# 256 rows of w_out loaded apart, on engines' queues of their own, in a decode step of attention and a gated MLP

## The chip, the cores and the metric

One core of a Trainium2 chip runs the whole kernel. The metric is the time of one execution on the device, in microseconds; the median of three runs is given, and one execution was taken apart by the hardware profiler. All times below are microseconds, from the start of the profiled span, unless ns is written.

## What is computed

One token `x` (576 numbers) is normalised; an attention block and a gated MLP read the same normalised row, and both results are added to `x`. Cut to what matters:

```
xn = layernorm(x)                                # 1 x 576
# A: 32 query heads on 16 key/value heads, the last 4096 of 65536 positions, heads of 128
q = xn @ wq;  p = softmax(q k^T / sqrt(128));  o = p v
a = o @ wo                                       # 4096 -> 576
# B: gated MLP; w_in is 576 x 4608, w_out is 2304 x 576
z = gelu(xn @ w_in);  z1, z2 = halves of z       # 2304 each
g = w_sp * layernorm(z2) + b_sp                  # w_sp and b_sp are single numbers here
b = (z1 * g) @ w_out
out = x + a + b
```

All inputs are bfloat16. Every weight and every cache row is read once: 51 MB for one row of 576 numbers.

## The kernel before

The heads are taken in four groups of four. For each group b, `turn(b)` transposes the keys on VectorE (eight instructions, L214), `scores(b)` multiplies them with the queries, finds the maximum and takes the exponential (L259 to L285), and `weigh(b)` and `heads(b)` sum the values (L293 to L307). The order is written out by hand at the end of the kernel: turn, scores and values of groups 0 to 2 interleaved, then `turn(3)`, `scores(3)`, `z_all`, `weigh(2)`, `gate`, `heads(2)`, then the first output products, `values(3)`, and the rest of the output products.

The big loads are all issued by SyncE (SP), in this order: `wq` in two, `k0`, `k1`, `v0`, `k2`, `v1`, `k3`, `win`, `v2`, `v3`, `wo` in two, `w_out` in four. They go into two pools of two buffers each, so that a load is issued when the tile that held its buffer has been read: `wo` waits for `win` (read by `z_all`), the tile `wout` for `k3` (read by `turn(3)`). An engine's instructions, the loads that it issues included, run in the order written. A load is split over DMA engines; sixteen serve this core.

`w_out` has 2304 rows; row f needs element f of the hidden vector `hv`. The kernel puts 2304 - 128 = 2176 of them on 128 partitions, 17 rows (FR) on each, and SP loads these in four pieces of 8, 6, 2 and 1 rows per partition (L124). The other 128 rows (FE) stand in further columns of the same tile. ScalarE loads them: 96 rows on 12 partitions, eight rows each (L382), and 32 rows on 32 partitions, one each (L383). Those 96 rows are read so that partition 4i + x gets the rows of block i of the x-th quarter.

`z_all` computes `xn @ w_in` as 9 accumulation steps. In each, eight matmuls write four groups of 32 PSUM partitions, two tiles; the elements that belong to the separate rows stand ahead of the first group's. VectorE copies the result to `zs` and transposes blocks of 32x32, so that each element comes to the partition that holds its row of `w_out` (L333 to L338). GpSimd clears the unused part of `zs` and of `zt`. `gate` then makes `hv`.

The output is one row, built in two PSUM tiles by matmuls with a single column as weights: `row_of` adds one column of `hv` (or of the attention's output `o_p`) times the matching 576 numbers, two matmuls of 288 each (L394). It is called for `x`, then for the columns of the separate rows, then, after `values(3)`, for the 32 columns of `wo`, and last for the 17 columns of `w_out`. Then come two copies and two stores of half a row each.

Of the kernel before, what the change touches and what calls it, by code (L numbers as in the profile page):

```python
# [8 lines left out]
FP32 = mybir.dt.float32  # L9
# [5 lines left out]
P = 128  # L15
D = 576
# [5 lines left out]
FH = 2304  # L22
# [6 lines left out]
NR = 9  # L29
EPS = 1e-5  # L30
SCALE = DH ** -0.5
GELU_C = 0.7978845608028654
FE = P
FR = (FH - FE) // P
FX = 8
FB = 12 * FX
FC = FR + FX + 1
FQ = P * FR // 4
FW = FQ // 2
WR = HQ * DH // P  # L40
HW = D // 2
ZPAD = 24
# [6 lines left out]
def kernel(  # L49
# [14 lines left out]
    nc = tc.nc  # L64
    ctx.enter_context(tc.manual_schedule())

    const = ctx.enter_context(tc.tile_pool(name="const", bufs=1))
    work = ctx.enter_context(tc.tile_pool(name="work", bufs=2))
    one = ctx.enter_context(tc.tile_pool(name="one", bufs=1))
# [7 lines left out]
    ps_a = ctx.enter_context(tc.tile_pool(name="ps_a", bufs=2, space=PS))  # L77


    x_row = const.tile([1, D], BF16, name="x_row")  # L80
    nc.scalar.dma_start(x_row[:], A_x.flatten_outer_dims())
    ws2 = const.tile([1, 2], BF16, name="ws2")
    nc.scalar.dma_start(ws2[:, 0:1], B_w_sp.flatten_outer_dims()[0:1, 0:1])
    nc.scalar.dma_start(ws2[:, 1:2], B_b_sp.flatten_outer_dims()[0:1, 0:1])
# [3 lines left out]
    def unit(name, width):  # L88
        pool = small if width == SMALL else large
        return pool.tile([P, width], BF16, name=name, tag="u")  # L90
# [4 lines left out]
    def load(t, view, width, cuts):  # L95
        for a, e in zip(cuts, cuts[1:]):
            nc.sync.dma_start(t[:, (a - cuts[0]) * width:(e - cuts[0]) * width], view[:, a * width:e * width])
# [19 lines left out]
    win_t = unit("win", LARGE)  # L117
# [3 lines left out]
    wo_t = unit("wo", LARGE)  # L121
    load(wo_t, wo_v, D, (0, 20, WR))
    wout_t = unit("wout", SMALL)
    load(wout_t, B_w_out[FE:FH, :].rearrange("(p r) n -> p (r n)", r=FR), D, (0, 8, 14, 16, FR))  # L124


    ident = const.tile([P, P], BF16, name="ident")
# [1 line left out]
    xw = const.tile([P, NR, 32], BF16, name="xw")  # L129
# [91 lines left out]
    for r in range(NR):  # L221
        for g in range(4):
            nc.tensor.matmul(q_ps[32 * g:32 * g + 32, :], lhsT=xw[:, r, :],  # L223
                             rhs=wq_t[:, 2048 * r + 512 * g:2048 * r + 512 * (g + 1)],
                             start=r == 0, stop=r == NR - 1, tile_position=(0, 32 * g))
# [5 lines left out]
    for g in range(4):  # L231
        nc.tensor.matmul(qr[:, :, g, :], lhsT=rep4[:, g, :, :].rearrange("p n q -> p (n q)"),
                         rhs=qT[:, :, 0:2, :].rearrange("p a h e -> p h a e"), start=True, stop=True)
# [17 lines left out]
    def scores(b):  # L251
        sm = one.tile([P, 2, 512], FP32, name=f"sm{b}", tag="sm")
        mx = work.tile([P, 2], FP32, name=f"mx{b}", tag="mx")
        for kk in range(2):
            s_ps = ps_s.tile([P, 512], FP32, name=f"s{b}_{kk}", tag="s")
            for k4 in range(4):
                for ce in range(4):
                    c, e = divmod(ce, 2)
                    nc.tensor.matmul(s_ps[:], lhsT=zq[:, b, ce, ZPAD - 8 * k4:ZPAD - 8 * k4 + P],  # L259
                                     rhs=kt[b, 4 * kk + k4][:, c, :, e],  # L260
                                     start=k4 == 0 and ce == 0, stop=k4 == 3 and ce == 3)
            nc.vector.tensor_tensor_reduce(  # L262
                out=sm[:, kk, :].rearrange("p (n s) -> p n s", s=HB),
                in0=s_ps[:].rearrange("p (n s) -> p n s", s=HB),
                in1=cm[:].unsqueeze(1).to_broadcast([P, P, HB]), scale=SCALE, scalar=-3e38,
                op0=ALU.add, op1=ALU.max, accum_out=mx[:, kk:kk + 1])
        m1 = work.tile([P, 1], FP32, name=f"m1{b}", tag="m1")
        nc.vector.tensor_max(m1[:], mx[:, 0:1], mx[:, 1:2])  # L268
        tr = ps_m.tile([P, P], FP32, name=f"tr{b}", tag="m")
        nc.tensor.matmul(tr[:], lhsT=m1[:].to_broadcast([P, P]), rhs=ident_f[:], start=True, stop=True)  # L270
        m8 = work.tile([P, 8], FP32, name=f"m8{b}", tag="m8")
        nc.vector.tensor_reduce(out=m8[:], in_=tr[:].rearrange("p (a x) -> p x a", x=8), axis=AXX, op=ALU.max)  # L272
        mj = work.tile([P, 8], FP32, name=f"mj{b}", tag="mj")
        nm = work.tile([P, 1], FP32, name=f"nm{b}", tag="nm")
        nc.vector.tensor_tensor_reduce(out=mj[:], in0=m8[:], in1=sel8[:], scale=-1.0, scalar=0.0,  # L275
                                       op0=ALU.mult, op1=ALU.add, accum_out=nm[:])
        p = one.tile([P, 1024], BF16, name=f"p{b}", tag="p")
        l = work.tile([P, 1], FP32, name=f"l{b}", tag="l")
        nc.scalar.activation(p[:], sm[:].rearrange("p k n -> p (k n)"), ACT.Exp, bias=nm[:], accum_out=l[:])  # L279
        p_t[b] = work.tile([P, 2, 16, 32], BF16, name=f"pt{b}", tag="pt")  # L280
        nc.vector.transpose(p_t[b][:].rearrange("p k u m -> p (k u m)"), p[:])  # L281
        su = ps_m.tile([P, 8], FP32, name=f"su{b}", tag="m")
        nc.tensor.matmul(su[:], lhsT=l[:].to_broadcast([P, P]), rhs=sel8[:], start=True, stop=True)  # L283
        rms[b] = work.tile([P, 8], FP32, name=f"rm{b}", tag="rm")
        nc.vector.reciprocal(rms[b][:], su[:])  # L285
# [23 lines left out]
    def values(b):  # L309
        heads(b, weigh(b))  # L310


    hv = const.tile([P, FC], BF16, name="hv")

    zt = const.tile([P, FC, 32], FP32, name="zt")
    nc.gpsimd.memset(zt[:, FR:, :], 0.0)


    def z_all():
        zs = one.tile([P, FQ + 32 * (FX + 1)], FP32, name="zs", tag="sm")  # L320
        nc.gpsimd.memset(zs[0:32, FQ:], 0.0)
        zx = zs[0:32, FQ:].rearrange("p (r i) -> p r i", i=32)
        zp = [ps_a.tile([P, FE + FW], FP32, name=f"z{i}", tag="a") for i in range(2)]
        for r in range(NR):
            for g in range(4):
                for i in range(2):
                    lead = FE if g == 0 and i == 0 else 0
                    a = FE + FQ * g + FW * i - lead
                    nc.tensor.matmul(zp[i][32 * g:32 * g + 32, FE - lead:], lhsT=xw[:, r, :],  # L329
                                     rhs=win_t[:, FH * r + a:FH * r + a + lead + FW],  # L330
                                     start=r == 0, stop=r == NR - 1, tile_position=(0, 32 * g))
        for i in range(2):
            nc.vector.tensor_copy(zs[:, FW * i:FW * (i + 1)], zp[i][:, FE:])  # L333
        nc.vector.tensor_copy(zx[:, 0:FX, 0:12].rearrange("p r (i x) -> p r i x", x=4),
                              zp[0][0:32, 0:FB].rearrange("p (x i r) -> p r i x", x=4, i=3))
        nc.vector.tensor_copy(zx[:, FX, :], zp[0][0:32, FB:FE])
        nc.vector.transpose(zt[:, 0:FR, :], zs[:, 0:FQ].rearrange("p (i r) -> p r i", r=FR))
        nc.vector.transpose(zt[0:32, FR:, :], zx)  # L338
        return zt[:, :, 0:2]

    def gate(z):
        def t3(name):
            return const.tile([P, FC, 2], FP32, name=name)

# [8 lines left out]
        nc.vector.reciprocal(e[:], e[:])  # L353
        G = const.tile([P, 2, FC], FP32, name="G")
        nc.vector.tensor_mul(G[:].rearrange("p h c -> p c h"), e[:], z)
        sz = const.tile([P, 2], FP32, name="sz")
        nc.vector.tensor_reduce(out=sz[:, 0:1], in_=G[:, 1, :], axis=AXX, op=ALU.add)
        jz = const.tile([P, FC], FP32, name="jz")
        nc.vector.tensor_tensor_reduce(out=jz[:], in0=G[:, 1, :], in1=G[:, 1, :], scale=1.0, scalar=0.0,
# [3 lines left out]
        mz = rstd_of(sp[:], FH, "mz")  # L363
        gz = const.tile([P, FC], FP32, name="gz")
        nc.vector.tensor_scalar(out=gz[:], in0=G[:, 1, :], scalar1=mz[:, 0:1], scalar2=mz[:, 3:4],
# [12 lines left out]
    values(1)  # L378
    turn(3)

    e0 = D * (FR + FX)
    nc.scalar.dma_start(wout_t[0:12, D * FR:e0], B_w_out[0:FB, :].rearrange("(x i r) n -> i x (r n)", x=4, i=3))  # L382
    nc.scalar.dma_start(wout_t[0:32, e0:e0 + D], B_w_out[FB:FE, :])  # L383
    scores(3)
    z = z_all()
    pvs2 = weigh(2)
    gate(z)
# [4 lines left out]
    def row_of(col, w, start=False, stop=False):  # L392
        for g in range(2):
            nc.tensor.matmul(fin[g][32 * g:32 * g + 1, :], lhsT=col, rhs=w[:, HW * g:HW * (g + 1)],  # L394
                             start=start, stop=stop, tile_position=(0, 32 * g))

    row_of(one_bf[:, 0:1], x_row, start=True)
    for r, rows in [(FR + j, 12) for j in range(FX)] + [(FR + FX, 32)]:
        row_of(hv[0:rows, r:r + 1], wout_t[0:rows, D * r:D * (r + 1)])
    values(3)  # L400


# [48 lines left out]
```

## Time and profile before

| | us |
|---|---|
| median of 3 runs | 127.54 (127.38 to 127.61) |
| the profiled execution | 127.4 |
| its span, first to last instruction | 125.6 |
| TensorE busy / VectorE busy / ScalarE busy / GpSimd busy | 77.5 / 64.7 / 10.2 / 4.5 |
| bytes moved | 51.03 MB, mean 406 GB/s |
| granted TensorE clock, mean | 0.864 |

The page gives busy time per engine, the DMA queues (q1 is SP's, q10 ScalarE's, q8 and q14 carry instructions), the chain of work that ended last, and groups of like instructions. PE is TensorE, DVE VectorE, ACT ScalarE, POOL GpSimd, SP SyncE. A line of a timeline has the start, the length, the engine, the source line and operation, the tiles (written from read), the shapes, and in brackets the idle time before with what ended it.

### The profile page before, as it was taken

What the parts mean: (1) busy time and instruction counts of PE and PEld (TensorE: products, weight loads), DVE (VectorE), ACT (ScalarE), POOL (GpSimd) and SP (SyncE); (2) the same over time, 40 slices, a digit from 0 to 9 for tenths busy, and PEclk for the clock granted to TensorE, in tenths of its full rate; (3) what the DMA queues carried; (4) which work ended last, traced back from release to release, by engine and by line L of the source; (5) the groups of instructions that cost most, each with busy time, mean ns of one, the idle gap of its engine ahead of it and who ended that gap; (6) DMA issues with size and microseconds to landing.
All of it is one profiled execution on the core that took longest, in us unless ns stands there. A gap on an engine that the chain in (4) does not pass through costs nothing.

```text
span 125.6 us, 1352 instructions
## 1 busy us (share of the span) xinstructions
PE 77.5 (62%) x546; PEld 37.7 (30%) x550; DVE 64.7 (52%) x132; ACT 10.2 (8%) x19; POOL 4.5 (4%) x12
## 2 busy tenths in 40 slices
PE   3230550099922997385799274997397188749661
PEld 3110220033302342225334033342274063235340
DVE  6660032499648998322998445998326840010001
ACT  4010000000021000310000221000300210100001
POOL 8500000000000000000000000000100000000000
PEclk9999999999985599955579999599958975786999
DMA  4999899898998979999898999989898989999960
GB/s 120 506 438 438 365 470 470 365 501 365 470 459 378 485 344 490 407 428 490 355 490 365 508 423 428 423 384 490 358 462 372 487 359 444 448 395 423 396 249 0
DMA packets 2526, 51.03 MB, mean 406 GB/s; under 512 B 298, under 2 KB 461, under 8 KB 717
## 3 DMA queue, kind: packets, MB, share of 16 engines
q1 hardware_dynamic: 2450, 50.81, 94.9%
q10 hardware_dynamic: 71, 0.15, 0.3%
q8 instruction: 4, 0.07, 0.2%
q14 instruction: 1, 0.01, 0.0%
HBM read 50.96 MB, written 0.00 MB: 406 GB/s over the span
## 4 chain that ended last, share of the span: by engine, by line
PE 42%; DMA 37%; DVE 11%; ACT 5%; issue 2%; SPq 1%; ACTq 0%
PE s L259 29%; DMA wout<-in_B_w_out_dram 20%; DMA k<-in_A_k_cache_dram 18%; ACT p L279 4%; PE pv L293 4%; DVE kt L214 4%; PE z L329 4%; PE op L304 2%; DVE sm L262 2%; PE tr L270 2%; PE fin L394 1%; DVE pt L281 1%; DVE m L272 1%; ACT pvs L298 1%; PE su L283 1%
## 5 line engine op out<-in xcount | busy, mean ns | idle before, releaser
L259 PE MATMUL s<-kt,zq 128*128 128x512 bf16 x124 | 36.3, 451 | 11.6 <-DVE kt L214 10.8
L214 DVE STREAM_TRANSPOSE kt<-k 128x1024 f32<-128x1024 f32 x32 | 36.4, 1204 | 3.9 <-DMA k<-in_A_k_cache_dram 3.9
L259 PEld LDWEIGHTS <-zq 128*128 128x128 bf16 x128 | 14.5, 113 | 32.4 <-issue 21.4
L293 PE MATMUL pv<-v,pt 128*32 128x512 bf16 x128 | 10.1, 469 | 1.1 <-DMA v<-in_A_v_cache_dram 1.1
L279 ACT ACTIVATE p<-sm,nm 128x1024 bf16<-128x1024 f32 x4 | 4.6, 1148 | 71.9 <-DVE nm L275 71.9
L223 PE MATMUL q_ps<-wq,xw 128*32 128x512 bf16 x36 | 4.2, 627 | 7.2 <-DMA wq<-in_A_wq_dram 4.9
L307 DVE TENSOR_TENSOR o_t<-op,rm 128x8 bf16<-128x8 f32 x4 | 0.7, 164 | 15.1 <-PE op L304 15.1
L281 DVE STREAM_TRANSPOSE pt<-p 128x1024 bf16<-128x1024 bf16 x4 | 5.0, 1245 | 5.4 <-ACT p L279 5.4
L262 DVE CUSTOM_DVE_ANT_1 sm<-s,cm 128x512 f32<-128x512 f32 x8 | 5.4, 671 | 3.5 <-PE s L259 3.5
L304 PE MATMUL op<-selu,pvs 128*128 128x8 f32 x32 | 5.3, 293 | 2.5 <-ACT pvs L298 2.1
L283 PE MATMUL su<-sel,l 128*128 128x8 f32 x8 | 1.8, 293 | 7.6 <-ACT p L279 7.6
L394 PE MATMUL fin<-wo,o_p 128*1 128x288 bf16 x64 | 5.7, 345 | 1.2 <-DMA wo<-in_A_wo_dram 1.1
L304 PEld LDWEIGHTS op<-selu,pvs 128*128 128x128 f32 x32 | 5.0, 236 | 4.6 <-ACT pvs L298 4.2
L418 DVE CAST res<-fin 1x288 bf16<-1x288 f32 x1 | 0.4, 445 | 11.4 <-PE fin L394 11.4
L394 PE MATMUL fin<-wout,hv 128*1 128x288 bf16 (+2 forms) x52 | 4.8, 336 | 2.3 <-DMA wout<-in_B_w_out_dram 2.2
L293 PEld LDWEIGHTS <-pt 128*32 128x32 bf16 x128 | 3.7, 112 | 5.8 <-issue 3.1
L227 DVE CAST q_sb<-q_ps 128x512 bf16<-128x512 f32 x1 | 0.7, 690 | 8.1 <-PE q_ps L223 8.1
L394 PEld LDWEIGHTS <-o_p 128*1 128x1 bf16 x64 | 3.3, 99 | 4.0 <-issue 1.1
L329 PE MATMUL z<-win,xw 128*32 128x272 bf16 (+1 forms) x72 | 4.4, 396 | 0.0
L270 PE MATMUL tr<-ident_f,m 128*128 128x128 f32 x8 | 2.0, 326 | 3.9 <-DVE m L268 3.9
L223 PEld LDWEIGHTS <-xw 128*32 128x32 bf16 x36 | 1.4, 130 | 9.2 <-issue 9.2
L298 ACT COPY pvs<-pv 128x512 f32<-128x512 f32 x4 | 2.3, 585 | 20.2 <-PE pv L293 20.2
(93 smaller groups left out, 41.8 us busy)
## 6 DMA issues: line engine op xcount, KB each, us to landing
k<-in_A_k_cache_dram SPq DMA_DIRECT2D x4, 4096.0 KB
v<-in_A_v_cache_dram SPq DMA_DIRECT2D x4, 4096.0 KB, 29.2
win<-in_B_w_in_dram SPq DMA_DIRECT2D x1, 5184.0 KB
wq<-in_A_wq_dram SPq DMA_DIRECT2D x1, 3584.0 KB, 12.7
wo<-in_A_wo_dram SPq DMA_DIRECT2D x1, 2880.0 KB
wo<-in_A_wo_dram SPq DMA_DIRECT2D x1, 1728.0 KB, 20.8
wout<-in_B_w_out_dram SPq DMA_DIRECT2D x1, 1152.0 KB
wq<-in_A_wq_dram SPq DMA_DIRECT2D x1, 1024.0 KB, 4.7
```

The lines of the kernel that those rows point to most:

```text
L214: nc.vector.transpose(t[:].rearrange("p c n e -> p (c n e)").bitcast(FP32), kn[b][:, UK * DH * k:UK * DH * (k + 1)].bitcast(FP32).rearrang ...
L223: nc.tensor.matmul(q_ps[32 * g:32 * g + 32, :], lhsT=xw[:, r, :], rhs=wq_t[:, 2048 * r + 512 * g:2048 * r + 512 * (g + 1)], start=r == 0, ...
L259: nc.tensor.matmul(s_ps[:], lhsT=zq[:, b, ce, ZPAD - 8 * k4:ZPAD - 8 * k4 + P], rhs=kt[b, 4 * kk + k4][:, c, :, e], start=k4 == 0 and ce = ...
L262: nc.vector.tensor_tensor_reduce(out=sm[:, kk, :].rearrange("p (n s) -> p n s", s=HB), in0=s_ps[:].rearrange("p (n s) -> p n s", s=HB), in ...
L270: nc.tensor.matmul(tr[:], lhsT=m1[:].to_broadcast([P, P]), rhs=ident_f[:], start=True, stop=True)
L279: nc.scalar.activation(p[:], sm[:].rearrange("p k n -> p (k n)"), ACT.Exp, bias=nm[:], accum_out=l[:])
L281: nc.vector.transpose(p_t[b][:].rearrange("p k u m -> p (k u m)"), p[:])
L293: nc.tensor.matmul(pv[32 * g:32 * g + 32, :].rearrange("p (n d) -> p n d", n=4), lhsT=p_t[b][:, kk, u, :], rhs=v4[:, kk, u, :, :], start=k ...
L298: nc.scalar.copy(pvs[:], pv[:])
L304: nc.tensor.matmul(op[:], lhsT=pvs[:, DH * u:DH * (u + 1)], rhs=selu[:, 8 * u:8 * u + 8], start=u == 0, stop=u == 3)
L329: nc.tensor.matmul(zp[i][32 * g:32 * g + 32, FE - lead:], lhsT=xw[:, r, :], rhs=win_t[:, FH * r + a:FH * r + a + lead + FW], start=r == 0, ...
L394: nc.tensor.matmul(fin[g][32 * g:32 * g + 1, :], lhsT=col, rhs=w[:, HW * g:HW * (g + 1)], start=start, stop=stop, tile_position=(0, 32 * g))
```

## The change

- SP's part of `w_out` shrinks from 17 to 16 rows per partition (pieces of 8, 5, 2 and 1), and 256 rows are loaded apart from it.
- ScalarE still loads 96 rows on partitions 0 to 11, eight rows each, but issues this after the exponential of `scores(3)`. Its 32-row load is gone.
- GpSimd loads 160 rows on partitions 64 to 79, ten rows each. Ahead of it and behind it GpSimd issues a short load (`skip`) of 8 and of 4 neighbouring partitions into columns that nothing reads. Before these it clears the ten columns of the separate rows on all 128 partitions.
- The products of the separate rows use all 128 partitions (ten columns), where they used 12 or 32 (nine columns).
- `z_all` has six matmuls in a step instead of eight: four of 512 columns, one of 96 and one of 160. VectorE's copies and transposes follow the new layout.
- `x_row` is loaded in two halves.

```diff
-FE = P
-FR = (FH - FE) // P
-FX = 8
-FB = 12 * FX
-FC = FR + FX + 1
-FQ = P * FR // 4
-FW = FQ // 2
+FR = 16
+FA, RA = 96, 8
+FB, RB = 160, 10
+FE = FA + FB
+FC = FR + RB
+FQ = 512
...
-    nc.scalar.dma_start(x_row[:], A_x.flatten_outer_dims())
+    for a in range(0, D, D // 2):
+        nc.scalar.dma_start(x_row[:, a:a + D // 2], A_x.flatten_outer_dims()[:, a:a + D // 2])
...
-    load(wout_t, B_w_out[FE:FH, :].rearrange("(p r) n -> p (r n)", r=FR), D, (0, 8, 14, 16, FR))
+    load(wout_t, B_w_out[FE:FH, :].rearrange("(p r) n -> p (r n)", r=FR), D, (0, 8, 13, 15, FR))
...
-    zt = const.tile([P, FC, 32], FP32, name="zt")
-    nc.gpsimd.memset(zt[:, FR:, :], 0.0)
...
-        zs = one.tile([P, FQ + 32 * (FX + 1)], FP32, name="zs", tag="sm")
-        nc.gpsimd.memset(zs[0:32, FQ:], 0.0)
+        zs = one.tile([P, FQ + 32 * RB], FP32, name="zs", tag="sm")
+        nc.gpsimd.memset(zs[:, FQ:], 0.0)
...
+        def product(i, g, r, a, n, to):
+            nc.tensor.matmul(zp[i][32 * g:32 * g + 32, to:to + n], lhsT=xw[:, r, :],
+                             rhs=win_t[:, FH * r + a:FH * r + a + n],
+                             start=r == 0, stop=r == NR - 1, tile_position=(0, 32 * g))
...
+                product(0, g, r, FE + FQ * g, FQ, 0)
+            product(1, 0, r, 0, FA, 0)
+            product(1, 2, r, FA, FB, FA)
+        nc.vector.tensor_copy(zs[:, 0:FQ], zp[0][:])
+        for q, n, a, rows, k in ((0, 12, 0, RA, 3), (64, 16, FA, RB, 4)):
+            nc.vector.tensor_copy(
+                zx[q:q + 32, 0:rows, 0:n].rearrange("p r (i x) -> p r i x", x=4),
+                zp[1][q:q + 32, a:a + n * rows].rearrange("p (x i r) -> p r i x", x=4, i=k))
+        zt = one.tile([P, FC, 32], FP32, name="zt", tag="zt")
         nc.vector.transpose(zt[:, 0:FR, :], zs[:, 0:FQ].rearrange("p (i r) -> p r i", r=FR))
-        nc.vector.transpose(zt[0:32, FR:, :], zx)
+        nc.vector.transpose(zt[:, FR:, :], zx)
...
-    e0 = D * (FR + FX)
-    nc.scalar.dma_start(wout_t[0:12, D * FR:e0], B_w_out[0:FB, :].rearrange("(x i r) n -> i x (r n)", x=4, i=3))
-    nc.scalar.dma_start(wout_t[0:32, e0:e0 + D], B_w_out[FB:FE, :])
+    def blocks(a, e, k):
+        return B_w_out[a:e, :].rearrange("(x i r) n -> i x (r n)", x=4, i=k)
+
+    def skip(k, a):
+        nc.gpsimd.dma_start(wout_t[0:k, a:a + 32].rearrange("i (m c) -> i m c", m=2),
+                            B_w_out[0:2 * k, 0:16].rearrange("(m i) n -> i m n", m=2))
+
+    nc.gpsimd.memset(wout_t[:, D * FR:D * FC], 0.0)
+    skip(8, D * FC)
+    nc.gpsimd.dma_start(wout_t[64:80, D * FR:D * FC], blocks(FA, FE, 4))
+    skip(4, D * FC + 32)
     scores(3)
+    nc.scalar.dma_start(wout_t[0:12, D * FR:D * (FR + RA)], blocks(0, FA, 3))
...
-    for r, rows in [(FR + j, 12) for j in range(FX)] + [(FR + FX, 32)]:
-        row_of(hv[0:rows, r:r + 1], wout_t[0:rows, D * r:D * (r + 1)])
+    for r in range(FR, FC):
+        row_of(hv[:, r:r + 1], wout_t[:, D * r:D * (r + 1)])
```

More of the change, by code (lines that the diff above doesn't have):

```diff
@@ L313 @@
     hv = const.tile([P, FC], BF16, name="hv")
-    zt = const.tile([P, FC, 32], FP32, name="zt")
-    nc.gpsimd.memset(zt[:, FR:, :], 0.0)
     def z_all():
-        zs = one.tile([P, FQ + 32 * (FX + 1)], FP32, name="zs", tag="sm")
-        nc.gpsimd.memset(zs[0:32, FQ:], 0.0)
-        zx = zs[0:32, FQ:].rearrange("p (r i) -> p r i", i=32)
-        zp = [ps_a.tile([P, FE + FW], FP32, name=f"z{i}", tag="a") for i in range(2)]
+        zs = one.tile([P, FQ + 32 * RB], FP32, name="zs", tag="sm")
+        nc.gpsimd.memset(zs[:, FQ:], 0.0)
@@ L324, in z_all @@
+        zx = zs[:, FQ:].rearrange("p (r i) -> p r i", i=32)
+        zp = [ps_a.tile([P, FQ], FP32, name=f"z{i}", tag="a") for i in range(2)]
+        def product(i, g, r, a, n, to):
+            nc.tensor.matmul(zp[i][32 * g:32 * g + 32, to:to + n], lhsT=xw[:, r, :],
+                             rhs=win_t[:, FH * r + a:FH * r + a + n],
+                             start=r == 0, stop=r == NR - 1, tile_position=(0, 32 * g))
         for r in range(NR):
             for g in range(4):
[L326 to L336, printed above, removed]
+                product(0, g, r, FE + FQ * g, FQ, 0)
+            product(1, 0, r, 0, FA, 0)
+            product(1, 2, r, FA, FB, FA)
+        nc.vector.tensor_copy(zs[:, 0:FQ], zp[0][:])
```

## The prediction

> **What bounds the kernel now.** I read the chain that ended last, then the queues, then the DMA share over the last microseconds, then the packets themselves. The end of the chain:
>
> ```profile
> 96.78 24.82 DMA wout<-in_B_w_out_dram
> 121.60 0.04 issue
> 121.64 1.43 PE fin L394 x18
> 123.07 0.43 DVE res L418
> ```
>
> The last loads of `w_out` end it, after them come 18 matmuls, a copy and the store. The queues:
>
> ```profile
> q1 hardware_dynamic: 2450, 50.81, 94.9%
> q10 hardware_dynamic: 71, 0.15, 0.3%
> q8 instruction: 4, 0.07, 0.2%
> q14 instruction: 1, 0.01, 0.0%
> ```
>
> SP's queue fills 95% of sixteen engines; ScalarE's carries 0.15 MB. So the end is set by bytes per engine, and by the fullest engine. The end of the stream, in columns us, busy time by engine, clock, DMA share, GB/s:
>
> ```profile
> 119.00:120.00 1.00, 0.49 (x9) 0.35 (x9) 0.00 (x0) 0.00 (x0) 0.00 (x0) 1.00 0.95 387
> 120.00:120.50 0.50, 0.50 (x12) 0.35 (x7) 0.00 (x0) 0.00 (x0) 0.00 (x0) 1.00 1.04 403
> 120.50:121.00 0.50, 0.16 (x4) 0.00 (x0) 0.00 (x0) 0.00 (x0) 0.00 (x0) 1.00 0.58 224
> 121.00:121.40 0.40, 0.00 (x0) 0.00 (x0) 0.00 (x0) 0.00 (x0) 0.00 (x0) 1.00 0.56 213
> 121.40:121.80 0.40, 0.16 (x4) 0.12 (x5) 0.00 (x0) 0.00 (x0) 0.00 (x0) 1.00 0.41 150
> 121.80:122.20 0.40, 0.40 (x10) 0.30 (x8) 0.00 (x0) 0.00 (x0) 0.00 (x0) 1.00 0.33 115
> ```
>
> From 120.5 the share is about a half: some engines are done while others still carry rows that the end waits for. The trace records the sixteen completions of the very last load (one per engine):
>
> ```
> 120.98 121.13 121.16 121.20 121.26 121.28 121.29 121.30 | 121.87 | 122.34 122.50 122.53 122.58 122.62 122.65 122.69
> ```
>
> Eight are early, one is 0.6 late, seven are 1.1 to 1.4 late. The packet records (start, duration, queue, size) say why, because on an engine one packet starts 3 to 4 ns before the last one ends and can be followed. Three late ones carry the `w_out[0:96]` load of L382: twelve packets of 9216 bytes, in three groups of four, which put their engines 1.42 behind (end of `v3` 105.04 against 103.63). Four others each carried one 16 KB packet of q8 (at 42.4, 77.7, 97.5, 116.4; 1.02 to 1.11 us each) and are 1.4 behind since then. The one at 121.87 carried q14's 8 KB packet at 38.6.
>
> **The change, part by part** (engine time, which is what counts here; 9216 bytes take 0.349, so 26.4 bytes per ns).
> - SP's `w_out` goes from 17 to 16 rows per partition: eight packets per engine shrink by 1152 bytes, 8 x 0.044 = 0.35 less on every engine.
> - The 32-row load of L383 goes. It put two 1152-byte packets on every engine: `v2`'s eight packets took 9.98 on engines with nothing else, `v3`'s, behind them, 9.71. So 0.27 less on each.
> - ScalarE's 96 rows stay four packets of 9216 bytes on three engines: nothing gained, nothing lost there.
> - GpSimd's 160 rows: the source is read as 4 of 4, where the 96 rows are read as 3 of 4 and went to three engines; so I take four engines with four packets of 11,520 bytes. 4 x 0.436 = 1.74 by bytes; 1.42 x 1.25 = 1.78 by the measured delay. The trace has no load issued by GpSimd; below, it costs its engines 0.44 each (spread over sixteen), above, 1.78.
> - The two `skip` loads: 32-byte pieces, two per partition; a 1152-byte packet lasts 0.051, so at most 0.1, on engines that have 0.3 to spare in the sum below.
>
> Sum, if those four engines are among the eight early ones: 121.28 - 0.35 - 0.27 + 1.74 = 122.40. The instruction engines come to 122.69 - 0.62 = 122.07, ScalarE's to 121.9. So the last completion moves from 122.69 to 122.40. Call SP's four loads of `w_out` a (8 rows per partition), b (5 after, 6 before), c (2) and d (1). Behind b come 16 matmuls instead of 18 (0.077 each); b lands 1.09 before d (121.60, 122.69 before), so 16 x 0.077 = 1.23 from 121.35 ends at 122.58, and d's last two at 122.40 + 0.33 = 122.73. Before, both ended at 123.02. The gain is 0.29. The profiled run took 127.4 (span 125.6, 1.8 around it); 127.4 - 0.29 = 127.11. The median is 0.14 above that run, so 127.25.
>
> Edits costed at nothing, with their cover:
> - `x_row` in two loads: one issue more on ACT (0.23 to 0.53). The matmuls of L161 start later than 2.05, but their copy waits for DVE until 4.20, and q_ps then waits 4.9 for `wq`. Without that cover it costs the issue time. The extra load shifts which semaphore each load takes: SP's `v0` now waits for the first half of `x_row` (landed at 2.00, `v0` is issued at 2.97), and d for `v2` (landed by 95.9) instead of ScalarE's load (96.9); all are there before SP comes to them.
> - `z_all`: 54 matmuls instead of 72 with the same 20,736 columns (4.4 before); copies and transposes on DVE 2.8 before, about 2.9 after. It releases `win`, on which SP's next load waits (95.44), and the queue still holds `v3` until 103.5: 8 us of cover. The 36 instructions fewer on PE put the fourth q8 packet about 1.5 later; its engine is still busy then.
> - GpSimd's memset of 128x5760 (L391 after): 128x2432 took 2.12 and 128x288 0.34, so 4.9, from 86.1 (when DVE has read `k3`) to 91.0. Queued behind it on GpSimd: three load issues and the memset of `zs`, for which DVE's copies wait; and ScalarE's load (86.12 before), behind which its next work is at 97.98.
>
> The fin matmuls on the separate rows now wait for GpSimd's load, and PE queues in order behind them:
>
> ```profile
> 102.95 2.31 PE L394 MATMUL fin<-wout,hv 12*1 12x288 bf16 x18
> 105.69 3.34 PE L293 MATMUL pv<-v,pt 128*32 128x512 bf16 x32 [0.42 <-DMA v<-in_A_v_cache_dram]
> 112.54 5.78 PE L394 MATMUL fin<-wo,o_p 128*1 128x288 bf16 x64 [1.09 <-DMA wo<-in_A_wo_dram]
> ```
>
> ScalarE's load before was issued at 86.12, its first packet moved at 91.00, its last ended at 95.2, since packets of q1 and q10 alternate. With an issue at 93 the same lag and four turns of 1.65 give 103 to 104 for GpSimd's. PE can stand more: `o_p` is ready at 111.7, 5.78 and 1.15 (the first 16 of `w_out`) lead to 118.6, and load b comes at 121.3. So 2.6 to spare beside `v3` (105.69), and the separate rows may start as late as 105.9.
>
> **Weighed against the row.** DVE can be held by GpSimd:
>
> ```profile
> 1.33 2.39 DVE L140 CAST ident_f<-ident 128x128 f32<-128x128 bf16 x1 [0.20 <-POOL ident masks.py:199]
> 1.52 2.12 POOL L138 MEMSET zq<- 128x2432 bf16 x1
> 3.96 0.32 DVE L156 COPY twice<-ident 64x128 bf16<-64x128 bf16 x1
> ```
>
> The cast took 2.39 and ended 0.08 after the memset, where a copy of the same width took 0.32. The new memset is twice as long and lies over `scores(3)` on DVE (L262 to L275, 87.2 to 89.2); at worst these wait until 91.0, 3 us, which the spare 2.6 and the wait for `v3` just about take. [...]
>
> **The rivals.**
> 1. *The load meets a loaded engine* (the other side). The trace names no engines. If one of the four is an instruction engine (122.58 to 122.69) it ends at 122.69 - 0.62 + 1.74 = 123.81, so 128.66: 1.1 slower. With the q14 engine, 121.87 - 0.62 + 1.74 = 122.99: 127.84. It decides from an engine that is over 0.3 behind the early ones. For: five of the thirteen engines without ScalarE's rows are loaded, and four taken anywhere miss them with 70/715. Against: the first load starts on eight engines at 1.76 to 1.88 and on the others at 2.06 to 2.47. Followed from there, the q14 engine, the q8 engine of 97.5 and one of ScalarE's three are in the first group, five of six early engines that can be followed are in the second; and ScalarE's first engine, which had just moved `x_row`, may be late for that reason. So the loaded ones look like one half of the engines, and a block that starts after a skip of eight lies in the other.
> 2. *The load is spread over sixteen engines*, and the four engines are not what happens. Then each gets 11,520 bytes, 0.44: 122.69 - 0.62 + 0.44 = 122.51, 127.36. For: the other loads with many partitions use all engines. Against: the 96 rows went to three. [...]
> 3. *The load comes late.* [...] Completion at 108 gives 129.4. For: 2 us of margin over an issue that the trace has never shown. [...]
>
> **How the numbers follow.** Forecast 0.63, rival 1 0.17, rival 2 0.07, rival 3 0.13. The measurement can tell 0.2%, 0.26 us. The forecast's own range is 126.9 (the instruction engines at 122.07 bind, and nothing else: 0.62 less) to 127.55 (1.78, and 0.2 for small packets); its centre is just past 0.2%, so I split it 0.39 faster, 0.22 same, 0.02 slower. Rival 2 is 0.02 and 0.05. Rivals 1 and 3 are slower. Sum: 0.41, 0.27, 0.32. For 8 in 10 the range has to take in rival 1: 126.9 to 128.7; rival 3 stays out.
>
> **What would show it.** Right: four packets of 11,520 bytes on each of four engines, last completions of the last load near 122.4 on these and 122.1 on the instruction engines, DMA share high until about 121.5. Wrong: completions at 123.7 (rival 1), sixteen such packets on sixteen engines (rival 2), or a long wait of PE for `wout` before `values(3)` (rival 3).

## The result, and the profile after

The median went from 127.56 (127.36 to 127.81, 7 runs) to 127.06 us (126.97 to 127.11, 7 runs): ratio 0.9961, 95% interval 0.9949 to 0.9973, a gain of 0.50. The profiled execution took 127.1 with a span of 125.3, so 0.3 less than the one of before. Measured again later, the pair gave 127.21 against 127.62, ratio 0.9966 (0.9954 to 0.9978), a gain of 0.41. The forecast was 127.25 (126.9 to 128.7), a gain of 0.29.

The queues of the changed kernel, with packets, MB and share of sixteen engines:

```profile
q1 hardware_dynamic: 2450, 50.66, 94.7%
q0 software_dynamic: 144, 0.19, 0.4%
q10 hardware_dynamic: 25, 0.11, 0.2%
q8 instruction: 4, 0.07, 0.2%
q14 instruction: 1, 0.01, 0.0%
```

SP's queue gave up 0.15 MB, the new queue q0 is GpSimd's, and the instruction packets of q8 and q14 are still there. The end of the chain:

```profile
98.28 23.00 DMA wout<-in_B_w_out_dram
121.32 1.40 PE fin L406 x16
122.72 0.44 DVE res L430
```

Still the loads of `w_out`, now 0.32 earlier (121.32 against 121.64), and 16 matmuls behind them. The end of the stream by windows, columns as before:

```profile
119.00:120.00 1.00, 1.00 (x20) 0.68 (x16) 0.00 (x0) 0.00 (x0) 0.00 (x0) 1.00 0.99 388
120.00:120.50 0.50, 0.50 (x12) 0.35 (x7) 0.00 (x0) 0.00 (x0) 0.00 (x0) 1.00 0.73 279
120.50:121.00 0.50, 0.19 (x4) 0.00 (x0) 0.00 (x0) 0.00 (x0) 0.00 (x0) 1.00 0.74 286
121.00:121.40 0.40, 0.08 (x2) 0.08 (x3) 0.00 (x0) 0.00 (x0) 0.00 (x0) 1.00 0.69 259
121.40:121.80 0.40, 0.40 (x8) 0.27 (x9) 0.00 (x0) 0.00 (x0) 0.00 (x0) 1.00 0.40 138
121.80:122.20 0.40, 0.40 (x8) 0.17 (x4) 0.00 (x0) 0.00 (x0) 0.00 (x0) 1.00 0.05 14
```

From 120.5 to 121.4 the share is 0.74 and 0.69, where it was 0.58 and 0.56: fewer engines are done early; the last window falls from 0.33 to 0.05. The sixteen completions of the very last load, one per engine:

```
120.48 120.56 120.71 120.72 | 121.31 | 121.70 121.75 121.90 121.98 122.10 122.13 122.14 122.26 122.29 122.30 122.35
```

Eight early engines have become four, and the last is at 122.35 (122.69 before; 122.40 was forecast). The other part of the change, on PE and GpSimd (start, length, work, idle before):

```profile
105.93 2.08 PE L406 MATMUL fin<-wout,hv 128*1 128x288 bf16 x16 [1.68 <-DMA wout<-in_B_w_out_dram]
113.97 5.68 PE L406 MATMUL fin<-wo,o_p 128*1 128x288 bf16 x64 [0.28 <-DVE o_p L420]
119.54 1.15 PE L406 MATMUL fin<-wout,hv 128*1 128x288 bf16 x16
121.32 1.36 PE L406 MATMUL fin<-wout,hv 128*1 128x288 bf16 x16 [0.63 <-DMA wout<-in_B_w_out_dram]
...
87.72 4.90 POOL L391 MEMSET wout<- 128x5760 bf16 x1 [83.19 <-DVE kt L214]
...
87.59 0.65 DVE L262 CUSTOM_DVE_ANT_1 sm<-s,cm 128x512 f32<-128x512 f32 x1
88.81 0.69 DVE L262 CUSTOM_DVE_ANT_1 sm<-s,cm 128x512 f32<-128x512 f32 x1 [0.56 <-PE s L259]
```

PE now waits 1.68 for GpSimd's load and has little to spare later (0.63 in front of load b). DVE's maxima under the memset take 0.65 and 0.69, as they did without it (0.65 and 0.69 in before).

### The profile page after: what moved, and what is told of

Its sections match the earlier page's. It is cut to its first block, busy times and chain, and to the rows that moved or that the text cites. A ratio compares the mean times of both kernels' runs of the same rounds, so it can differ in the third digit from the quotient of the medians.

```text
span 125.3 us, 1324 instructions
## 1 busy us (share of the span) xinstructions
PE 77.9 (62%) x528; PEld 39.3 (31%) x532; DVE 65.0 (52%) x131; ACT 10.2 (8%) x19; POOL 11.0 (9%) x15
## 4 chain that ended last, share of the span: by engine, by line
PE 43%; DMA 36%; DVE 10%; ACT 4%; issue 3%; SPq 1%; ACTq 0%
PE s L259 29%; DMA wout<-in_B_w_out_dram 18%; DMA k<-in_A_k_cache_dram 18%; PE pv L293 4%; DVE kt L214 4%; PE z L323 3%; ACT p L279 3%; PE op L304 2%; DVE sm L262 2%; PE tr L270 2%; PE fin L406 1%; PE su L283 1%; DVE pt L281 1%; DVE m L272 1%; ACT pvs L298 1%
## 5 line engine op out<-in xcount | busy, mean ns | idle before, releaser
L259 PE MATMUL s<-kt,zq 128*128 128x512 bf16 x124 | 36.8, 458 | 11.8 <-DVE kt L214 11.1
L259 PEld LDWEIGHTS <-zq 128*128 128x128 bf16 x128 | 14.5, 113 | 33.0 <-issue 22.4
L391 POOL MEMSET wout<- 128x5760 bf16 x1 | 4.9, 4897 | 83.2 <-DVE kt L214 83.2
L293 PE MATMUL pv<-v,pt 128*32 128x512 bf16 x128 | 11.9, 498 | 0.0
L293 PEld LDWEIGHTS <-pt 128*32 128x32 bf16 x128 | 5.7, 119 | 3.8 <-issue 2.4
L406 PE MATMUL fin<-wout,hv 128*1 128x288 bf16 x52 | 5.1, 344 | 2.3 <-DMA wout<-in_B_w_out_dram 2.3
L161 PE MATMUL x_ps<-one_bf,x_row 1*64 1x1 bf16 x9 | 1.2, 248 | 5.6 <-DMA x_row<-in_A_x_dram 5.6
L323 PE MATMUL z<-win,xw 128*32 128x512 bf16 (+2 forms) x54 | 4.4, 448 | 0.0
L406 PEld LDWEIGHTS <-hv 128*1 128x1 bf16 x52 | 2.6, 95 | 4.5 <-issue 3.0
## 6 DMA issues: line engine op xcount, KB each, us to landing
wo<-in_A_wo_dram SPq DMA_DIRECT2D x1, 1728.0 KB, 19.4
```

What stands on the lines that cost most here:

```text
L293: nc.tensor.matmul(pv[32 * g:32 * g + 32, :].rearrange("p (n d) -> p n d", n=4), lhsT=p_t[b][:, kk, u, :], rhs=v4[:, kk, u, :, :], start=k ...
L323: nc.tensor.matmul(zp[i][32 * g:32 * g + 32, to:to + n], lhsT=xw[:, r, :], rhs=win_t[:, FH * r + a:FH * r + a + n], start=r == 0, stop=r = ...
L391: nc.gpsimd.memset(wout_t[:, D * FR:D * FC], 0.0)
```

## The experiments

Two theories: the end is set by the fullest engine, and GpSimd's four engines are ones that have nothing else (the sum of the prediction); against it, that the four would do as well anywhere, or that something else, not the bytes per engine, carries the gain. Engine numbers are not in the trace: they are counted here from the order of GpSimd's loads, each taken to start on the engine after the last one's. This is the author's assumption, which no trace shows by itself. The packets of the change fit it: eight of 64 bytes (and eight of 8) in the first short load, four groups of the rows, four of 64 bytes (and twelve of 8) in the second. That would make sixteen engines in all, and each execution would start at the same one. An instruction engine is one that carries a 16 KB packet of q8. Each ratio is against the kernel before, measured beside it.

**Which four engines.** First the four after four (e1), then the four after twelve (e2):

```diff
-    skip(8, D * FC)
-    nc.gpsimd.dma_start(wout_t[64:80, D * FR:D * FC], blocks(FA, FE, 4))
     skip(4, D * FC + 32)
+    nc.gpsimd.dma_start(wout_t[64:80, D * FR:D * FC], blocks(FA, FE, 4))
+    skip(8, D * FC)
```

> The changed kernel with its GpSimd loads in another order: the short one of 4, then the 160 rows, then the short one of 8. Same bytes, same partitions, same queues; if the short loads place the long one, its four engines are now the fifth to eighth. Theory (the fullest engine sets the end): the engines with instruction packets get 1.74 more, last completion near 123.8 instead of 122.35, time 128.5 (128.3 to 128.8), four of the sixteen completions near 120.6 become eight. Rival (a third queue helps wherever its load falls): 127.06 as before, the same completions.

Measured: 130.76, ratio 1.0244 (1.0229 to 1.0259). The direction was expected, the size not: 2.3 more than 128.5. All engines ended 2 us later than in the change: fourteen at 122.52 to 124.42, where the change has 120.48 to 122.35, and two, which fit instruction engines, at 125.80 and 125.92. The rows themselves moved slowly: GpSimd's packets of 11,520 bytes took up to 0.64 instead of 0.434, ScalarE's of 9216 up to 0.68 instead of 0.349, and SP's packets ran at 19.4 to 22.4 bytes per ns from 96 to 104, where they ran at 26.9 until then.

```diff
     skip(8, D * FC)
-    nc.gpsimd.dma_start(wout_t[64:80, D * FR:D * FC], blocks(FA, FE, 4))
     skip(4, D * FC + 32)
+    nc.gpsimd.dma_start(wout_t[64:80, D * FR:D * FC], blocks(FA, FE, 4))
```

> The changed kernel with both short loads ahead of the 160 rows, so that its engines are the last four. Theory: these are as empty as the four before them, last completion 122.2 to 122.4, time 127.05 within 0.15. Rival (partitions 64 to 79 have engines of their own, and others write them slower): packets of 11,520 bytes longer than 0.434 and a time over 127.3.

Measured: 130.93, ratio 1.0260 (1.0244 to 1.0275). A miss of 3.9 us, and the rival came: packets of 11,520 bytes took up to 0.79, and all engines ended late (122.62 to 125.03, and two at 126.05 and 126.08). How much of this comes from engines that aren't empty is told apart in e5.

**Without the rows (e3), and with more of them (e4).**

```diff
-    nc.gpsimd.dma_start(wout_t[64:80, D * FR:D * FC], blocks(FA, FE, 4))
```

> The changed kernel without the load of the 160 rows (they count as zero; a short load of 4 takes its place). Theory: eight engines complete near 120.5 to 120.7 and idle, the instruction engines bind at 122.1 to 122.3, time 126.85 to 127.05: the load that it leaves out costs 0.0 to 0.2, though it is 184 KB. Rival (the load or its memset and wait on PE is what sets the new time): 126.5 or less.

Measured: 127.05 (126.87 to 127.2), ratio 0.9953 (0.9938 to 0.9968). Eight engines are early again (120.44 to 120.71) and the last is at 122.44. So the 160 rows cost nothing that can be measured (127.05 without them, 127.06 with them): they lie on engines that would wait anyway.

```diff
-FR = 16
+FR = 15
-FB, RB = 160, 10
+FB, RB = 288, 9
...
-    nc.gpsimd.memset(wout_t[:, D * FR:D * FC], 0.0)
...
-    nc.gpsimd.dma_start(wout_t[64:80, D * FR:D * FC], blocks(FA, FE, 4))
-    skip(4, D * FC + 32)
+    nc.gpsimd.dma_start(wout_t[64:96, D * FR:D * FC], blocks(FA, FE, 8))
+    nc.gpsimd.memset(wout_t[0:64, D * FR:D * FC], 0.0)
```

> 384 rows apart: 96 by ScalarE as in the change, 288 by GpSimd on partitions 64 to 95, nine rows each, read as 8 of 4, so on eight engines with four packets of 10,368 bytes; SP's part is 15 rows per partition. GpSimd's load is issued ahead of the memset, which covers partitions 0 to 63 only, and the products use 96 partitions. Theory: every engine loses another 0.35, the eight early ones get 1.57: last completion 121.8 to 122.0, time 126.6 to 126.75. Rival (PE's chain behind the separate rows is next: it had 0.6 left in the changed kernel): 126.9 or more, with load b of w_out landing before PE comes to it.

Measured: 128.34, ratio 1.0059 (1.0041 to 1.0077): slower, a miss. Here the packets were not stretched (10,368 bytes in 0.39 to 0.40), and fourteen engines ended by 122.24; two ended at 123.27 and 123.55, and two were done at 120.26 and 120.58. That fits two instruction engines among the eight after eight: 122.07 of the prediction, 0.35 less for the 16th row, four packets of 0.393 more make 123.3.

**Engine or partition.** The first two runs changed the engines and left the rows on partitions 64 to 79 (packets of up to 0.64 and 0.79), the fourth used eight engines and partitions 64 to 95 (0.39 to 0.40). The expectations of e5 and e6 take it that each engine has partitions that it writes in the 128-partition loads: 80 to 95 for the four engines after twelve, and so 64 to 79 for the four after eight. The packet records name neither engines nor partitions, so this is an assumption of the author's. Two runs cross engine and partition: e5 is e2 with partitions 80 to 95, e6 is the change with partitions 80 to 95 (the diff of e6; e5 has the same on top of e2).

```diff
-        for q, n, a, rows, k in ((0, 12, 0, RA, 3), (64, 16, FA, RB, 4)):
+        for q, n, a, rows, k, c in ((0, 12, 0, RA, 3, 0), (64, 16, FA, RB, 4, 16)):
...
-                zx[q:q + 32, 0:rows, 0:n].rearrange("p r (i x) -> p r i x", x=4),
+                zx[q:q + 32, 0:rows, c:c + n].rearrange("p r (i x) -> p r i x", x=4),
...
-    nc.gpsimd.dma_start(wout_t[64:80, D * FR:D * FC], blocks(FA, FE, 4))
+    nc.gpsimd.dma_start(wout_t[80:96, D * FR:D * FC], blocks(FA, FE, 4))
```

> GpSimd's loads in the order skip 8, skip 4, load (as in the run in which the load came last), but the 160 rows on partitions 80 to 95 instead of 64 to 79. Theory: a load issued by GpSimd runs at full rate when each engine writes the partitions that it also writes in the 128-partition loads (the four engines after twelve: 80 to 95 on the upper half), and stretches otherwise. Then the 11,520-byte packets are back at 0.43 to 0.44 us, no slice of the bandwidth between 97 and 107 falls under 380 GB/s, and what is left is that two of these four engines carried an instruction packet: last completion 122.1 + 1.74 = 123.8, time 128.5. Rival (the place in the order, last on the queue, is what slows): 130.9 as before, packets of 0.5 to 0.8.

> GpSimd's loads in the order of the change (skip 8, load, skip 4), but the 160 rows on partitions 80 to 95 instead of 64 to 79: the same engines, other partitions. Theory (an engine that writes partitions of another engine stretches its packets and everybody's): 11,520-byte packets of 0.5 to 0.8 us, all completions about 2 us later, time 129 to 131. Rival (only the engines matter, not the partitions): packets of 0.434, time 127.06 as the change.

Measured: e5 128.88 (1.0105, 1.0090 to 1.0120), e6 129.31 (1.0134, 1.0107 to 1.0161). The four kernels, two windows each (last column GB/s), first the change (engines after eight, partitions 64 to 79):

```profile
101.00:104.00 3.00, 1.57 (x12) 1.43 (x12) 1.75 (x10) 0.50 (x2) 0.00 (x0) 0.94 0.98 417
104.00:107.00 3.00, 1.32 (x12) 0.65 (x12) 0.55 (x3) 0.00 (x0) 0.00 (x0) 0.50 1.00 423
```

e6 (same engines, partitions 80 to 95):

```profile
101.00:104.00 3.00, 1.00 (x8) 0.94 (x8) 1.67 (x9) 0.55 (x3) 0.00 (x0) 1.00 1.02 327
104.00:107.00 3.00, 0.74 (x6) 0.40 (x5) 0.86 (x4) 0.19 (x1) 0.00 (x0) 0.55 1.03 313
```

e2 (engines after twelve, partitions 64 to 79):

```profile
101.00:104.00 3.00, 2.50 (x12) 2.15 (x12) 1.53 (x10) 0.50 (x2) 0.00 (x0) 0.62 0.99 325
104.00:107.00 3.00, 0.06 (x2) 0.00 (x0) 0.00 (x0) 0.00 (x0) 0.00 (x0) 0.50 0.96 278
```

e5 (engines after twelve, partitions 80 to 95):

```profile
101.00:104.00 3.00, 1.35 (x10) 1.29 (x10) 1.75 (x10) 0.50 (x2) 0.00 (x0) 0.98 0.88 376
104.00:107.00 3.00, 0.42 (x3) 0.08 (x2) 0.74 (x4) 0.00 (x0) 0.00 (x0) 0.50 1.05 444
```

The DMA share is about full in all of them (the 376 of e5 comes with 0.88); the bytes are not. Engine and partition together decide: eight with 64 to 79 and twelve with 80 to 95 move 376 to 444 GB/s, the two crossed pairs 278 to 327. The packets say the same:

| engines after | partitions | 11,520-byte packet, median (longest) | SP's packets, 102 to 106, bytes per ns | last completion | time |
|---|---|---|---|---|---|
| eight (the change) | 64 to 79 | 0.434 (0.441) | 26.8 to 26.9 | 122.35 | 127.06 |
| eight (e6) | 80 to 95 | 0.546 (0.788) | 20.4 to 20.5 | 124.45 | 129.31 |
| twelve (e5) | 80 to 95 | 0.434 (0.441) | 26.8 to 26.9 | 124.00 | 128.88 |
| twelve (e2) | 64 to 79 | 0.551 (0.791) | 18.5 to 20.5 | 126.08 | 130.93 |

The four kernels come out as the assumption has it: packets of 0.434 in the two pairs that it takes to match, 0.546 and 0.551 in the crossed ones. Why the crossed writes are slow, no run here shows. In e5 only two engines were late, at 123.83 and 124.00 (123.8 expected). Followed in the packet records, as in the prediction, the two engines that are last at the end of `wo`'s first part (113.61 and 113.78, the others by 112.15) carry four of GpSimd's packets each and the instruction packets at 79.4 and 39.1. That its time is 0.4 over the expected 128.5 comes from PE, since its load came last on the queue:

```profile
116.99 7.76 PE fin L406 x96
124.75 0.43 DVE res L430
...
108.30 2.08 PE L406 MATMUL fin<-wout,hv 128*1 128x288 bf16 x16 [3.88 <-DMA wout<-in_B_w_out_dram]
```

The chain ends on PE, not on a load. From 108.30 PE ran to 124.75 without a wait for a load, 16.45 us. By that a start at 105.93 ends at 122.38, and the change ended at 122.72: 0.34 was left of the cover. In e6 and e2 the chain ends on PE too (starts at 108.69 and 110.39), so their last completions say more of the loads than their times.

**More engines, six on partitions 64 to 87 (e7).** ScalarE 144 rows, GpSimd 240 on six engines, SP 15 rows per partition:

```diff
-FR = 16
-FA, RA = 96, 8
-FB, RB = 160, 10
+FR = 15
+FA, RA = 144, 12
+FB, RB = 240, 10
...
-    nc.gpsimd.dma_start(wout_t[64:80, D * FR:D * FC], blocks(FA, FE, 4))
-    skip(4, D * FC + 32)
+    nc.gpsimd.dma_start(wout_t[64:88, D * FR:D * (FR + RB)], blocks(FA, FE, 6))
+    skip(2, D * FC + 32)
+    nc.gpsimd.memset(wout_t[64:96, D * (FR + RB):D * FC], 0.0)
+    nc.gpsimd.memset(wout_t[0:64, D * FR:D * FC], 0.0)
```

> 384 rows apart instead of 256, SP 15 rows per partition: ScalarE's load 144 rows (12 each on 12 partitions, three engines), GpSimd's 240 rows (10 each on partitions 64 to 87, six engines, issued ahead of the memsets). SP's part is 0.35 us less per engine than in the change; GpSimd's six engines carry four packets of 11,520 bytes each, ScalarE's three carry packets of 13,824 bytes. If the two engines added to the four are early ones: GpSimd's engines 122.35 - 0.35 = 122.0, instruction engines 121.8, ScalarE's 121.9 - 0.35 + 0.71 = 122.2; last completion 122.2, time 126.9. If one or both carry an instruction packet: 121.8 + 1.74 = 123.5, time 128.3. Third: as many rows on engines, but later, so that PE waits: over 127.5 with a wait of PE for wout ahead of values(3).

Measured: 128.43, ratio 1.0073 (1.0046 to 1.0101), the second case: one engine at 123.48, the others by 122.27. That engine can be followed too: it carries the instruction packet at 39.0 and four of GpSimd's. So one of the two added engines is an instruction engine. Packets kept their length (0.435 in the median), as in the change and e5 (0.434). The third case came with it, through ScalarE's load: issued at 96.42, behind GpSimd's two memsets (89.43 to 91.76) and 4.60 of its sequencer in the chain, it landed at 106.89. PE began the separate rows at 107.03 and ended at 123.85, about where 123.48 would have put it as well.

**The 32 rows of L383.** In before, SP's packets run at 24.4 to 24.6 bytes per ns from 91 to 93 (24.9 to 25.2 from 92 to 94 in its second profile), while this load's packets land on partitions 0 to 31 from all sixteen engines. One run takes it from the kernel before (e9), one adds a like one to the change (e11):

```diff
-    nc.scalar.dma_start(wout_t[0:32, e0:e0 + D], B_w_out[FB:FE, :])
+    nc.gpsimd.memset(wout_t[0:32, e0:e0 + D], 0.0)
```

> The kernel before without the load of L383: the 32 rows aren't read (32 of the 2304 rows are left out of the sum; GpSimd clears their columns instead). In the traces of before, all of SP's packets run at 24.4 to 25 bytes per ns instead of 26.9 for 3 to 3.5 us while this load's 1152-byte packets land on partitions 0 to 31 from all sixteen engines; no other stretch before 110 does that. Theory (writes from foreign engines stretch everybody's packets): without it no such dip at 91 to 95, last completion earlier by 0.09 (bytes: 2304 per engine) + 0.25 (8% of 3.5 us) = 0.3, time 127.3. Rival (the dip comes from ScalarE's 96 rows, or from nothing that this load does): bytes alone, 0.09, time 127.5, the dip stays.

```diff
     nc.scalar.dma_start(wout_t[0:12, D * FR:D * (FR + RA)], blocks(0, FA, 3))
+    nc.scalar.dma_start(wout_t[0:32, D * FC + 64:D * (FC + 1) + 64], B_w_out[0:32, :])
```

> The change with a load like that of L383 added behind ScalarE's: 32 rows on partitions 0 to 31, one each, into columns that nothing reads. Theory (foreign writes from all sixteen engines stretch everybody's packets by some 8% for 3.5 us): a dip of SP's packets to about 24.5 bytes per ns where it lands, 0.09 + 0.25 = 0.3 later, time 127.4. Rival (bytes alone): 0.09, time 127.15, no dip.

Measured: e9 127.43, ratio 0.9987 (0.9978 to 0.9996), so 0.05 to 0.28 faster, under the 0.3 expected. The dip is gone (26.9 to 27.0 from 91 to 95): it is this load's. The mean of the last load's sixteen completions, less the mean landing of `wq`'s first part, is 116.57 and 116.50 in the two profiles of before and 116.23 here, 0.3 less as expected; the median time, set by the fullest engine, got 0.12 of it. e11 took 127.94 against 127.06 and 127.21 of the change; its dip is at 24.6 from 97 to 98 and 25.8 from 98 to 99, the same mean is 0.31 later, and the last completion is at 122.83, 0.48 later. Its time rose by 0.7 to 0.9. The trace shows where the rest lies: the last store lands 0.51 later than in the change (124.92 against 124.41), and the span ends 0.79 later. At the end SP waits for the semaphores of all loads and stores one after another; with the load added it comes to a store's in its second wait, from 124.10 to 124.95, and has five more to go through, where the change meets the stores in its last two.

**x_row in one load (e10).**

```diff
-    for a in range(0, D, D // 2):
-        nc.scalar.dma_start(x_row[:, a:a + D // 2], A_x.flatten_outer_dims()[:, a:a + D // 2])
+    nc.scalar.dma_start(x_row[:], A_x.flatten_outer_dims())
```

> The change with x_row in one load as before. The second half landed at 5.44 and made the first matmuls 3.4 us later, but q_ps still waited 2.4 us for wq. Theory (hidden): the wait of q_ps for wq grows by 3.4 us, the time stays at 127.06, within 0.2%. Rival (it also moved something on the queue or the semaphores that counts): off by over 0.25 us.

Measured: 127.23 (127.12 to 127.41), ratio 0.9972 (0.9962 to 0.9982), within 0.2% of the change's 127.06 and 127.21. First the change, then this run:

```profile
5.57 1.17 PE L161 MATMUL x_ps<-one_bf,x_row 1*64 1x1 bf16 x9 [5.57 <-DMA x_row<-in_A_x_dram]
14.07 0.62 PE L223 MATMUL q_ps<-wq,xw 128*32 128x512 bf16 x4 [2.39 <-DMA wq<-in_A_wq_dram]
```

```profile
2.07 1.20 PE L160 MATMUL x_ps<-one_bf,x_row 1*64 1x1 bf16 x9 [2.07 <-DMA x_row<-in_A_x_dram]
14.07 0.62 PE L222 MATMUL q_ps<-wq,xw 128*32 128x512 bf16 x4 [4.96 <-DMA wq<-in_A_wq_dram]
```

The first matmuls start 3.5 apart, `q_ps` goes on at 14.07 in both.

**Both kernels again (e8, e12).** The first measurement gave 0.50 by the medians and 0.34 by the profiles.

> The kernel before, unchanged. The median gain of the change was 0.50 us, that of the two profiled runs 0.34. If the first profile of before lies at the fast end of its spread, this one shows a span of 125.7 to 126.0 and a last completion of 122.8 to 123.1, and what is later in it tells where the spread comes from; if not, again 125.6 and 122.69.

> The change, unchanged. In the profiles so far the last completion of the last load less the slowest engine's landing of wq's first part (the first large load) is 117.26 and 117.27 in the two of before (122.69 - 5.43, 122.99 - 5.72), 116.80 in the change (122.35 - 5.55) and 116.83 with x_row whole. Theory (how late the slowest engine starts differs from run to run, 5.4 to 5.7, and everything behind it moves with it): again 116.75 to 116.85 whatever the start is, so a gain of 0.45 at equal starts; median 127.0 to 127.2. Rival (the start has nothing to do with it, the gain is the 0.34 of the first two profiles): last completion at 122.35 whatever the start is.

Measured: before again 127.72, span 125.9, last completion 122.99; it is 0.3 later from the first large load on (the slowest engine lands `wq`'s first part at 5.72, at 5.43 in the first profile). The change again 127.21 (126.97 to 127.25), last completion 122.39 with a slowest landing at 5.67: the difference is 116.72, not 116.75 to 116.85, and the rival's 122.35 is the nearer one. So the first profile of before, at 127.4, lay at the low end of its runs (127.36 to 127.81), which is why the profiles show less than the medians. Why a late start moves the end of before by 0.3 and that of the change by 0.04 was not settled.

## Why the prediction was right

- **The sum.** Last completion 122.40 forecast, 122.35 measured; profiled run 127.11 forecast, 127.1 measured. The step to the median (0.14 above the profiled run) was off: the medians of the change are 127.06 and 127.21, at its profiled runs (127.1 and 127.16). The sum started from a profile at the low end of before's runs, so the profiles differ by 0.34 where the medians differ by 0.50 and 0.41.
- **0.35 and 0.27 less on each engine.** Without the 160 rows (e3) the eight early completions are at 120.44 to 120.71, where before has 120.98 to 121.30: 0.54 to 0.65 less, near the 0.62. The instruction engines were put at 122.07; in e3 the last engine is at 122.44, 0.37 later than the sum has it. The slowest engine of e3 landed `wq`'s first part at 5.70, against 5.43 in before, which would be 0.27 of it. The 0.27 for the 32 rows is right as a mean (0.3 in e9) and 0.12 in the time. The prediction read it from `v2`'s packets, 9.98 against `v3`'s 9.71, and put it on two 1152-byte packets per engine; their bytes make 0.09, and e9 and e11 show the rest as stretched packets of SP's. No run takes the 17th row away by itself.
- **Which engines end last.** The sum put the four loaded engines at 122.40 and the instruction engines 0.33 ahead of them. Followed in the packet records of the change they are level: at the end of `wo`'s first part the four are at 111.91 to 112.11, three instruction engines at 111.75 to 112.05 (the fourth's packet comes at 118.7). So it is partly luck that 122.40 met 122.35: the engines that were to have 0.33 to spare end with the four.
- **1.74 more on four engines.** Sixteen packets in four groups of four, 0.433 to 0.441 each: 1.74. The prediction took this from the 96 rows, and rival 2 is out.
- **That the four are early ones.** True, but not for the reason given, so this was luck. The prediction took the loaded engines for one half and the engines from eight on for free. e5 shows two instruction engines among the last four, and e4 and e7 fit them. The four after eight are free; had the block been put four further, the same argument would have given it a good chance, and it was 3.9 us off (e2), or 1.8 on partitions 80 to 95 (e5). Rival 1's price was right: 123.81 forecast, 123.83 and 124.00 in e5.
- **What was not seen at all:** which partitions the rows stand on. The change was costed by bytes per engine alone, and by that e6 would be equal to the change; it is 2.2 slower.
- **The GpSimd load's landing** was put at 103 to 104 and came at 105.84: issued at 93.25, first packet at 99.67, a lag of 6.4 where ScalarE's had 4.9. It used up the cover of 2.6 almost to the end (0.34 left by e5). Rival 3 was nearer than 0.13 says: in e5 the separate rows start at 108.30, the chain ends on PE, and the time is 128.88. The packets show a cause that the prediction left out: GpSimd's queue moved its first packet at 96.85, 4.29 after its first issue, but the short load ahead of the rows has packets on all sixteen engines (its completions are at 98.55 to 99.67), and the rows come behind them, 2.8 after the first packet; in e5, behind two such loads, they come 5.3 after it (97.00 and 102.28). `skip` was costed as engine time, not as a turn in the queue.
- **x_row in halves** was costed at an issue, 0.53 at most, if not covered. The second half landed at 5.44 behind `wq`'s packets, 3.4 later than the whole row before. The miss was of a size; the cover (4.9, of which 2.4 is left) held, and e10 shows no effect.
- **The memset** was 4.90 as worked out, from 87.72 instead of 86.1, and did not hold DVE's maxima (0.65 and 0.69).

## What to carry to other kernels

Where loads bound a kernel, count the completions of the last load per engine. Here engines that ended early took 160 rows at no cost that could be measured (127.05 without them, 127.06 with them), in sixteen packets on four engines. Try the partitions too: with the loads in the same order the time was 127.06 with the rows on partitions 64 to 79 and 129.31 on 80 to 95 (e6). A load that feeds work in the middle needs its landing worked out, queue turns included: the rows came 2.8 after the queue's first packet behind one short load and 5.3 behind two (e5), and in e5 the chain ended on PE, at 124.75, and no longer on a load (last completion 124.00).

## What was not expected of the hardware

- Four packets on each of four engines, on partitions 80 to 95 where the change has 64 to 79, slowed SP's packets from 26.9 to 20.4 or 20.5 bytes per ns (102 to 106), and the three windows from 98 to 107 from 433, 417 and 423 GB/s to 374, 327 and 313, with the last completion 2.1 later for 184 KB (124.45 in e6, 122.35 in the change). A load of 36 KB spread over sixteen engines onto 32 partitions cost 4 to 9% of the rate for some 2 us (24.4 to 24.6 bytes per ns in before, 24.6 and 25.8 in e11, where 26.9 is the rate beside it).
- The instruction packets seem to stay on their engines while the instructions change: e4 (late engines at 123.27 and 123.55), e5 (123.83 and 124.00) and e7 (one at 123.48) all fit two of them on the last four engines and none on the four after eight, and e1's two late engines (125.80 and 125.92) fit the other two. This rests on the assumed count of engines.
